# Indirect DMAs of GpSimd in another order and apart, from the last routing steps to the second expert's gathers

## The chip, the cores and the metric

The kernel runs on one core of a Trainium2 chip. The metric is the device time of one execution in microseconds (us), and the profile is that of one execution. TensorE (PE) multiplies, VectorE (DVE), ScalarE (ACT) and GpSimd (POOL) work on tiles in on-chip memory, and SyncE (SP) issues most of the plain DMAs. GpSimd also issues the indirect DMAs, whose row numbers come from a tile in on-chip memory.

## The reference

Two stages. The first is linear attention with a decay per head, in 12 blocks of 64 positions for 4 batches and 8 heads of 64. Its output, as 3072 rows of 512, goes through eight experts, each row through the one with the largest gate logit:

```python
intra = np.einsum('bhij,bhjd->bhid', np.einsum('bhic,bhjc->bhij', qb, kb) * Dmask, vb)
inter = np.einsum('bhid,bhde->bhie', qb * lam_pow, kv_state)
...
e_idx = np.argmax(x @ w_gate, axis=1)
gate_w = probs[np.arange(N), e_idx]
eom = 1.0 / (1.0 + np.exp(-(x @ w_output_gate)))
for e in range(E):
    mask = e_idx == e
    h = np.maximum(x[mask] @ w1[e], 0.0)
    out[mask] = gate_w[mask, None] * eom[mask, e, None] * (h @ w2[e])
```

## The kernel before

**Attention.** The 3072 rows are 24 tiles of 128 (6 chunks of positions by 4 batches). A loop over `s` from −2 to 21 is a software pipeline: in turn `s`, tile `s`+2 is loaded and turned (`stage_a`), tile `s`+1 has its scores (`stage_b`, L392, masked by VectorE into `at`, L401), and tile `s` its outputs (`stage_c1`, L416, and `stage_c`, L436, evicted into `xT`, L443). The order of the work on each engine is the order of the code. Behind the loop a tail does the last tile.

**Routing.** Tiles are routed in groups of four, the last four in pairs (`RES` is 16, `LAST` 20). For a group, `logits` multiplies (L484), `logit_rows` turns the result (ScalarE's `lT`, L488, TensorE's L495, VectorE's `lg`, L499), `route_choose` finds the expert (`oh`, L592) and `route_place` the place of each row among its expert's rows: ranks by TensorE (`pr`, L629 to L642), ten small operations of VectorE, and the index and the record of each tile in a list `pending`. `place_scatter` (L703) takes tiles from that list and writes their records into the table `tab_d` by an indirect DMA each (L708). `mark` (L604) compares slots with places, for `found`, with which TensorE finds expert 0's rows without the table.

**Gathers.** `gather` (L954) fetches 128 blocks of rows of x by one indirect DMA (L960) into `xg`. An expert has 14 of them. Expert 0's gathers 0 to 7 hold rows of the tiles ahead of 16 alone; 8 to 13 hold the late ones and wait for `row_join`. `row_index` turns the loaded table (`load_rows`, SyncE) into row numbers. `x_turn` (L977) turns gathered blocks into `y`, which expert 0's up matmuls read (L1012, `fill` runs some of them between the tail's steps). The up matmuls are evicted by ScalarE (`hhi`, L1031). L84 to L86 are down products, whose weights ScalarE casts to `whi` (L130).

**What sets GpSimd's order.** GpSimd executes in the order of the code. An indirect DMA holds it for about 1 us. `pace(t)` (L881) is a copy of one element of `t`, by which GpSimd waits until `t` is written. In the loop's turns 18 to 21 a gather follows a `pace` on the turn's `at`, another a `pace` on its `xT`, and in some turns a scatter follows. After the tail's chain there are four scatters, six gathers, fourteen gathers of the second expert (ten at once, four in `next_rows`), two sends of finished rows (L1163) and the third expert's gathers.

Of the kernel before, what the change touches and what calls it, by code (L numbers as in the profile page):

```python
# [25 lines left out]
def kernel(  # L26
# [673 lines left out]

    pending = []

    def place_scatter(count):  # L703
        for _ in range(min(count, len(pending))):
            idx, rec = pending.pop(0)
            scatter(
                "table",
                nc.gpsimd.indirect_dma_start(  # L708
                    out=tab_d,
                    out_offset=bass.IndirectOffsetOnAxis(ap=idx, axis=0),  # L710
                    in_=rec,
                    in_offset=None,
                    bounds_check=P * E * EB - 1,
                    oob_is_err=False,
                ),
            )

    def scatter(group, ins):
        inst = getattr(ins, "ins", ins)
        tc.declare_no_dep(inst, group=group, reason="these scatters write different rows")  # L720
        tc.add_to_no_dep_group(group, inst)
# [159 lines left out]
    def pace(t):  # L881
        nc.gpsimd.tensor_copy(out=beat, in_=t)

    def row_index(p, j0=0):
        if p >= E:
            return
        t, n = idxs[(p, j0)]
        gf = const.tile([32, 4 * n], F32, name=f"rowf_{p}_{j0}")
        nc.vector.scalar_tensor_tensor(
            out=gf, in0=t[:, :, 2], scalar=float(4 * NT), in1=t[:, :, 2], op0=ALU.is_lt, op1=ALU.mult  # L890
        )
        gi = const.tile([P, 4 * n], I32 if p else F32, name=f"rows_{p}_{j0}")
        for qq in range(4):
            nc.vector.tensor_scalar(
                out=gi[32 * qq : 32 * qq + 32], in0=gf, scalar1=float(P * qq), scalar2=None, op0=ALU.add
            )
        if p == 0:
            part0[j0] = gi
            return
        for b in range(4 * n):  # L900
            gis[(p, 4 * j0 + b)] = gi[:, b : b + 1]
# [49 lines left out]

    xg = {}

    def gather(p, b0=0, b1=None, rows=NT):  # L954
        if p >= E:
            return
        for b in range(b0, NB[p] if b1 is None else min(b1, NB[p])):
            if (p, b // 4) not in xg:
                xg[(p, b // 4)] = slot(f"xg_{p}_{b // 4}")
            nc.gpsimd.indirect_dma_start(  # L960
                out=xg[(p, b // 4)][:, (b % 4) * P : (b % 4 + 1) * P],
                out_offset=None,
                in_=x_q[0 : 4 * rows],
                in_offset=bass.IndirectOffsetOnAxis(ap=gis[(p, b)], axis=0),
                bounds_check=4 * rows - 1,
                oob_is_err=False,
            )
# [301 lines left out]
    with tc.manual_schedule():  # L1269
# [13 lines left out]
        for s in range(-2, NTILE - 2):  # L1283
# [45 lines left out]
            if s == RES + 1:  # L1329
                weave(len(later))  # L1330
                expert_regs(0, order_i, 1)
                place_scatter(B // 2)
            if s >= RES + 2:
                if s > RES + 2:
                    pace(live[s + 1]["at"][1][0:1, 0, 0:1])
                gather(0, 2 * (s - RES - 2), 2 * (s - RES - 2) + 1, RES * P)
            if 0 <= n < LAST:
                stage_d2(n)
            if s in STORES:
# [29 lines left out]
                load_piece(0)  # L1369
            if s >= RES + 2:  # L1370
                pace(xTs[s][0:1, 256:257])
                gather(0, 2 * (s - RES - 2) + 1, 2 * (s - RES - 2) + 2, RES * P)
                if s < RES + 4:
                    place_scatter(1)
                if s == RES + 5:
                    load_rows(0, 2)
                    load_piece(1)
# [6 lines left out]
        stage_b(n)  # L1384
        weave(2)
        stage_b2(n)
        stage_c(n - 1)
        logits(LAST, 2)
        weave(len(later))
        for b in range(B):  # L1390
            mark(RES, b, 1, late_width)
        place_scatter(len(pending))
        stage_c1(n)
        logit_rows(LAST)
        stage_c(n)
        at_once(route_choose(LAST, LAST + 2))
        place = route_place(LAST, LAST + 2)
        place[0]()
        place[-1]()
        x_turn(0, 0)  # L1400
        logits(LAST + 2, 2)
        stage_d2(n - 3, 2)
        fill(8)
        x_turn(0, 1)
        logit_rows(LAST + 2)
        fill(8)
        at_once(route_choose(LAST + 2, NTILE))
        stage_d2(n - 1, 2)
        load_piece(2)
        load_piece(3)  # L1410
# [6 lines left out]
            last[i]()  # L1417
        for b in range(2):
            mark(LAST + 2, b, 1, late_width)
        for f in place[1:-1]:  # L1420
            f()
        place_scatter(len(pending))
        for b in range(2):
            mark(LAST, b, 1, late_width)
        fill(10)
        pfound = bank("pfound_late")
        for n in range(RES, NTILE):
            found(pfound, n, (n - RES) // B + 1, late_width, n == RES, n == NTILE - 1)
        for i in (1, 3, 5, *range(7, len(last))):
            last[i]()  # L1430
        place_scatter(len(pending))
        settle(1)
        row_index(0, 2)
        fill(2)
        row_turn(2, pfound, late_width)
        row_join(2, late_width)
        gather(0, 8)
        settle()
        sort_rest(counts)
        row_counts()  # L1440
# [8 lines left out]
        for j in range(4):  # L1449
            split_quarter(3, j)  # L1450
            if j == 0:
                row_index(1)
                gather(1, 0, 10)
            fill(2)
            settle()
        fill(4)
# [22 lines left out]
        for p in range(E):  # L1479
# [5 lines left out]
            for fc in range(NFC):  # L1485
                if p == 0:
                    up(p, fc, 1)
                    if fc >= 4:
                        next_split(4, (fc - 4,))
                        for f in work[:2]:  # L1490
                            f()
                        work = work[2:]
                else:
                    up(p, fc)
                    next_split(4 * p + 2, (fc,))

                    if fc == 1 and p in TURNED:
                        out_index(p)
                    if fc == 3 and p == 2:
                        count_over()  # L1500
                    if fc >= 4:
                        for f in work[: (fc - 2) // 2]:
                            f()
                        work = work[(fc - 2) // 2 :]
                if fc == 3 and p in TURNED:
                    down_banks(p)
                if p == 0 and fc < 2:
                    next_rows(1, 10 + 2 * fc, 12 + 2 * fc)
                if p == 0 and fc == 2:
                    for ids, yn in held:  # L1510
                        send_rows(ids, yn)
                if p > 0:
                    b = (4 * 2 if p - 1 in TURNED else 2 * 2) + fc
                    next_rows(p + 1, b, 14 if fc == NFC - 1 else b + 1, hts[(p, fc)][0][0:1, 0:1].bitcast(F32))
                if fc == 0:
                    load_outs(p + 1)
                    load_rows(p + 2)
                if p - 1 in TURNED:
                    if fc == 2:
                        fetch_turned(p - 1)  # L1520
                    if fc >= 5:
                        send_turned(p - 1, fc - 5)
# [183 lines left out]
```

## Time and profile before

| what | us |
|---|---|
| median of 3 runs | 437.83 |
| lowest and highest | 436.9 and 438.7 |
| profiled execution | 437.95 |
| span of its profile | 435.9 |
| TensorE busy in the span | 406.9 |
| GpSimd busy | 237.6 |
| VectorE busy | 289.6 |
| ScalarE busy | 183.8 |

The span is the time from the first to the last instruction in the profile. A line of a time line has a start, a length, the engine, the line of the code, the operation with the tile that it writes and those that it reads, and in brackets the engine's idle time before it with what ended it. "issue" there means that nothing the profile shows was waited for. The granted clock of TensorE is given as a share of 2.4 GHz.

### The profile page before, as it was taken

How to read it: one execution, taken by the hardware profiler on the slowest of the kernel's cores; microseconds unless marked ns; L12 is line 12 of the kernel's file. 1: busy time of each engine (PE TensorE's matmuls, PEld its weight loads, DVE VectorE, ACT ScalarE, POOL GpSimd, SP SyncE). 2: the span in 40 equal slices, each digit the busy share in tenths (PEclk: the TensorE clock that was granted, in tenths of full speed). 3: DMA queues.
4: the chain of work that ended last, by engine and by line, in shares of the span. 5: the costliest groups of instructions: out<-in, count | busy, mean ns of one | idle time of the engine just before them, and what ended most of it. 6: DMA issues, size and time to landing. Idle time of an engine off the chain costs nothing.

```text
span 435.9 us, 10864 instructions
## 1 busy us (share of the span) xinstructions
PE 406.9 (93%) x3847; PEld 376.2 (86%) x3847; DVE 289.6 (66%) x852; ACT 183.8 (42%) x450; POOL 237.6 (55%) x323
## 2 busy tenths in 40 slices
PE   8899999987959789699999999999999999999995
PEld 5788889775839568589999999999999999999984
DVE  3767668594737442396767995796796796895611
ACT  3766666564411220254532551460461470471400
POOL 2478886766341747337657755654755755702302
PEclk9999999998868969699999999999999999999999
DMA  9999789989515516544447884784695695683301
GB/s 190 234 232 245 206 219 252 220 219 269 170 43 162 161 25 228 177 114 155 132 137 225 225 294 143 207 283 167 164 339 188 165 337 198 158 326 139 97 32 46
DMA packets 106287, 81.99 MB, mean 188 GB/s; under 512 B 67029, under 2 KB 81387, under 8 KB 106211
## 3 DMA queue, kind: packets, MB, share of 16 engines
q1 hardware_dynamic: 97666, 67.52, 53.8%
q0 software_dynamic: 6288, 13.12, 9.7%
q8 instruction: 52, 0.85, 0.8%
q10 hardware_dynamic: 2256, 0.30, 0.5%
q14 instruction: 25, 0.20, 0.1%
HBM read 63.78 MB, written 17.55 MB: 187 GB/s over the span
## 4 chain that ended last, share of the span: by engine, by line
PE 86%; issue 4%; DMA 3%; DVE 2%; SPq 2%; ACT 1%; another core or an unknown queue 1%; POOL 0%; ACTq 0%; POOLq 0%
PE ph L831 27%; PE py L831 23%; PE ph L1012 6%; PE po L436 5%; PE ps L392 5%; PE po L416 3%; PE pyr L84 2%; PE pk L344 2%; PE pyr L85 2%; PE pyr L86 2%; DMA qkv<-in_q_dram 2%; PE pq L344 2%; PE pl L484 2%; PE pst L449 2%
## 5 line engine op out<-in xcount | busy, mean ns | idle before, releaser
L960 POOL DMA_INDIRECT xg<-x_d,rows x103 | 114.4, 1111 | 69.0 <-issue 38.5
L1031 ACT ACTIVATE hhi<-ph 128x400 fp32r<-128x400 f32 (+6 forms) x72 | 33.5, 469 | 146.5 <-PE ph L831 96.5
L139 DVE TENSOR_TENSOR wlo<-raw,whi 128x512 fp32r<-128x512 f32 x120 | 79.7, 684 | 0.1
L831 PE MATMUL ph<-xhi,whi 128*128 128x400 f32 (+4 forms) x224 | 75.7, 338 | 0.0
L831 PE MATMUL ph<-xhi,wlo 128*128 128x422 f32 (+6 forms) x224 | 75.4, 337 | 0.0
L831 PE MATMUL ph<-xlo,whi 128*128 128x422 f32 (+6 forms) x224 | 75.2, 336 | 0.0
L130 ACT CAST whi<-raw 128x512 fp32r<-128x512 f32 x120 | 70.2, 615 | 5.6 <-DMA raw<-in_moe_w_dram 5.3
L1037 DVE SCALAR_TENSOR_TENSOR hlo<-ph,hhi 128x400 fp32r<-128x400 f32 (+6 forms) x72 | 37.1, 519 | 49.7 <-ACT hhi L1031 24.7
L831 PE MATMUL py<-hhi,whi 128*128 128x400 f32 (+9 forms) x192 | 65.1, 339 | 0.0
L831 PE MATMUL py<-hhi,wlo 128*128 128x422 f32 (+5 forms) x192 | 65.0, 338 | 0.0
L831 PE MATMUL py<-hlo,whi 128*128 128x422 f32 (+5 forms) x192 | 64.9, 338 | 0.0
L401 DVE TENSOR_TENSOR at<-ps,decay 128x512 f32<-128x512 f32 x48 | 31.3, 684 | 28.3 <-PE ps L392 23.3
L831 PEld LDWEIGHTS ph<-xlo,whi 128*128 128x128 f32 x224 | 42.2, 188 | 0.2
L831 PEld LDWEIGHTS ph<-xhi,wlo 128*128 128x128 f32 x224 | 42.1, 188 | 0.2
L831 PEld LDWEIGHTS ph<-xhi,whi 128*128 128x128 f32 x224 | 42.1, 188 | 0.2
L708 POOL DMA_INDIRECT tab_d<-rec,idx x24 | 24.7, 1028 | 24.1 <-DVE marks L604 15.5
L831 PEld LDWEIGHTS py<-hlo,whi 128*128 128x128 f32 x192 | 36.1, 188 | 0.2
L831 PEld LDWEIGHTS py<-hhi,wlo 128*128 128x128 f32 x192 | 36.1, 188 | 0.2
L831 PEld LDWEIGHTS py<-hhi,whi 128*128 128x128 f32 x192 | 36.0, 188 | 0.1
L352 ACT COPY qT<-pq 64x256 f32<-64x256 f32 x88 | 34.6, 393 | 2.1 <-PE pq L344 1.3
L1012 PE MATMUL ph<-y,raw 128*128 128x128 f32 (+2 forms) x160 | 30.7, 350 | 4.4 <-issue 4.4
L1012 PEld LDWEIGHTS ph<-y,raw 128*128 128x128 f32 x160 | 27.5, 216 | 7.1 <-issue 6.3
(215 smaller groups left out, 677.9 us busy)
## 6 DMA issues: line engine op xcount, KB each, us to landing
raw<-in_moe_w_dram SPq DMA_DIRECT2D x32, 1024.0 KB
x_d<-xn SPq DMA_DIRECT2D x12, 512.0 KB
qkv<-in_k_dram SPq DMA_DIRECT2D x38, 128.0 KB
qkv<-in_v_dram SPq DMA_DIRECT2D x19, 256.0 KB
qkv<-in_q_dram SPq DMA_DIRECT2D x36, 128.0 KB
yd<-yo SPq DMA_DIRECT2D x17, 256.0 KB
yr<-yd SPq DMA_DIRECT2D x68, 64.0 KB
xg<-x_d,rows POOLq DMA_INDIRECT x103
```

Of the source, the lines that this page charges most:

```text
L130: nc.scalar.copy(out=hi, in_=src)
L139: eng.tensor_tensor(out=lo, in0=src, in1=hi.bitcast(F32), op=ALU.subtract)
L352: copies = [lambda r=r, view=view, src=src: nc.scalar.copy(out=view(qT[r]), in_=src) for r, view, src in query_parts(pq)]
L392: nc.tensor.matmul(L["ps"][y][t, m * P : (m + 1) * P], L["kT"][r, m, t], L["qT"][r, m, :], start=True, stop=True)
L401: nc.vector.tensor_tensor(out=at, in0=ps.rearrange("p (g t) -> p g t", g=NPAIR), in1=dec[:, j], op=ALU.mult)
L436: nc.tensor.matmul(po[j * D : (j + 1) * D, i * P : (i + 1) * P], vt[:, 4 * y + m, :], L["at"][y][:, m, :], start=(c == 0), stop=(c == 0 or ...
L708: nc.gpsimd.indirect_dma_start(out=tab_d, out_offset=bass.IndirectOffsetOnAxis(ap=idx, axis=0), in_=rec, in_offset=None, bounds_check=P * ...
L831: nc.tensor.matmul(ps[:, 0:m], a[x], b[y][:, 0:m], start=first and i == 0, stop=last and i == 2)
L960: nc.gpsimd.indirect_dma_start(out=xg[(p, b // 4)][:, (b % 4) * P : (b % 4 + 1) * P], out_offset=None, in_=x_q[0 : 4 * rows], in_offset=ba ...
L1012: nc.tensor.matmul(phs[(p, fc)][:, r].rearrange("p (b r) -> p b r", b=nb), raws[fc // 4][:, kc, sl], ys[(p, h)][:, y0 : y0 + nb * P].rearr ...
L1031: nc.scalar.activation(out=hi[:, r], in_=ph[:, r], func=AF.Relu)
L1037: nc.vector.scalar_tensor_tensor(out=to, in0=ph[:, r], scalar=0.0, in1=hi[:, r].bitcast(F32), op0=ALU.max, op1=ALU.subtract,)
```

## The change

`idle_for(n)` is new: `n` copies of one element of the constant tile `warm`. `place_scatter` and `gather` take a count `rests` and put so many ahead of each DMA. With it and with `pace` the order of the indirect DMAs is another:

- Turn 17 has no scatter. Turns 18 to 21 have one gather and one scatter each, in place of two gathers and, in turns 18 and 19, one scatter.
- Gathers 4 to 7 of expert 0 stand in the tail. Gathers 4, 5 and 7 each stand behind a pace, on tile 23's `at` and on the last two `xT`; gather 6 stands behind a copy.
- The four scatters of tiles 16 to 19 come after gather 7, each behind a copy.
- The rest of `route_place` for tiles 20 and 21, its two scatters and two marks come ahead of `stage_d2(n - 3, 2)`, and `row_index(0, 2)` ahead of the last `logit_rows`; `x_turn(0, 1)` goes behind the last `route_choose`.
- The last two scatters, gathers 8 to 13 of expert 0 and all fourteen of expert 1 have a copy ahead of each.

```diff
-    def place_scatter(count):
+    def place_scatter(count, rests=0):
         for _ in range(min(count, len(pending))):
             idx, rec = pending.pop(0)
+            idle_for(rests)
...
+    def idle_for(count):
+        for _ in range(count):
+            pace(warm[0:1])
...
-    def gather(p, b0=0, b1=None, rows=NT):
+    def gather(p, b0=0, b1=None, rows=NT, rests=0):
...
+            idle_for(rests)
...
             if s == RES + 1:
                 weave(len(later))
                 expert_regs(0, order_i, 1)
-                place_scatter(B // 2)
             if s >= RES + 2:
                 if s > RES + 2:
                     pace(live[s + 1]["at"][1][0:1, 0, 0:1])
-                gather(0, 2 * (s - RES - 2), 2 * (s - RES - 2) + 1, RES * P)
+                gather(0, s - RES - 2, s - RES - 1, RES * P)
...
                 pace(xTs[s][0:1, 256:257])
-                gather(0, 2 * (s - RES - 2) + 1, 2 * (s - RES - 2) + 2, RES * P)
-                if s < RES + 4:
-                    place_scatter(1)
+                place_scatter(1)
...
         stage_b2(n)
+        pace(live[n]["at"][1][0:1, 0, 0:1])
+        gather(0, 4, 5, RES * P)
         stage_c(n - 1)
+        pace(xTs[n - 1][0:1, 256:257])
+        gather(0, 5, 6, RES * P)
         logits(LAST, 2)
         weave(len(later))
         for b in range(B):
             mark(RES, b, 1, late_width)
-        place_scatter(len(pending))
+        gather(0, 6, 7, RES * P, 1)
         stage_c1(n)
         logit_rows(LAST)
         stage_c(n)
+        pace(xTs[n][0:1, 256:257])
+        gather(0, 7, 8, RES * P)
+        place_scatter(len(pending), 1)
         at_once(route_choose(LAST, LAST + 2))
...
         logits(LAST + 2, 2)
+        for f in place[1:-1]:
+            f()
+        place_scatter(len(pending), 1)
+        for b in range(2):
+            mark(LAST, b, 1, late_width)
         stage_d2(n - 3, 2)
         fill(8)
-        x_turn(0, 1)
+        row_index(0, 2)
         logit_rows(LAST + 2)
         fill(8)
         at_once(route_choose(LAST + 2, NTILE))
+        x_turn(0, 1)
...
-        for f in place[1:-1]:
-            f()
-        place_scatter(len(pending))
-        for b in range(2):
-            mark(LAST, b, 1, late_width)
         fill(10)
...
-        place_scatter(len(pending))
+        place_scatter(len(pending), 1)
         settle(1)
-        row_index(0, 2)
...
-        gather(0, 8)
+        gather(0, 8, rests=1)
...
-                gather(1, 0, 10)
+                gather(1, 0, 10, rests=1)
...
-                    next_rows(1, 10 + 2 * fc, 12 + 2 * fc)
+                    gather(1, 10 + 2 * fc, 12 + 2 * fc, rests=1)
```

GpSimd, from turn 17's scatters to turn 20, before (`rec` is the record of a tile, `rows_0` the row numbers of expert 0's first gathers; x2 stands for two alike in a row):

```order
L708 DMA tab_d<-rec_868,idx_1912 24576x3 x2
L361 TENSOR_TENSOR qd_2118<-qT_2098,qdec 128x512
L960 DMA xg_0_2165<-x_d,rows_0_2162 128x128
L882 COPY beat<-xT_2170 1x1
L960 DMA xg_0_2165<-x_d,rows_0_2162 128x128
L708 DMA tab_d<-rec_868,idx_1912 24576x3
L882 COPY beat<-at_1_2260 1x1
L960 DMA xg_0_2165<-x_d,rows_0_2162 128x128
L882 COPY beat<-xT_2267 1x1
L960 DMA xg_0_2165<-x_d,rows_0_2162 128x128
L708 DMA tab_d<-rec_868,idx_1912 24576x3
L882 COPY beat<-at_1_2365 1x1
```

and after:

```order
L361 TENSOR_TENSOR qd_2112<-qT_2092,qdec 128x512
L966 DMA xg_0_2159<-x_d,rows_0_2156 128x128
L883 COPY beat<-xT_2164 1x1
L709 DMA tab_d<-rec_868,idx_1912 24576x3
L883 COPY beat<-at_1_2251 1x1
L966 DMA xg_0_2159<-x_d,rows_0_2156 128x128
L883 COPY beat<-xT_2258 1x1
L709 DMA tab_d<-rec_868,idx_1912 24576x3
L883 COPY beat<-at_1_2353 1x1
L966 DMA xg_0_2159<-x_d,rows_0_2156 128x128
```

Each indirect DMA now stands behind a copy of its own that waits for data of the turn, and the scatters are one to a turn.

GpSimd, from the loop's last gathers into the tail, before (`rec_957` is of tiles 16 to 19, `rec_1193` and `rec_1284` are of the last two pairs):

```order
L882 COPY beat<-at_1_2469 1x1
L960 DMA xg_1_2384<-x_d,rows_0_2162 128x128
L882 COPY beat<-xT_2480 1x1
L960 DMA xg_1_2384<-x_d,rows_0_2162 128x128
L708 DMA tab_d<-rec_957,idx_2382 24576x3 x4
L708 DMA tab_d<-rec_1193,idx_2608 24576x3 x2
L708 DMA tab_d<-rec_1284,idx_2678 24576x3 x2
L960 DMA xg_2_2781<-x_d,rows_2_2778 128x128 x4
L960 DMA xg_3_2794<-x_d,rows_2_2778 128x128 x2
L960 DMA xg_0_2941<-x_d,rows_0_2936 128x128 x4
```

and after:

```order
L883 COPY beat<-at_1_2516 1x1
L966 DMA xg_1_2519<-x_d,rows_0_2156 128x128
L883 COPY beat<-xT_2523 1x1
L966 DMA xg_1_2519<-x_d,rows_0_2156 128x128
L883 COPY beat<-warm 1x1
L966 DMA xg_1_2519<-x_d,rows_0_2156 128x128
L883 COPY beat<-xT_2571 1x1
L966 DMA xg_1_2519<-x_d,rows_0_2156 128x128
L883 COPY beat<-warm 1x1
L709 DMA tab_d<-rec_957,idx_2370 24576x3
L883 COPY beat<-warm 1x1
L709 DMA tab_d<-rec_957,idx_2370 24576x3
```

Gathers 4 to 7 now stand ahead of the four scatters of tiles 16 to 19, and no two DMAs stand side by side.

VectorE, between the one-hot of tiles 20 and 21 and the logits of tiles 22 and 23, before (`y` is what `x_turn` writes, `xn` the turned `xT` that is stored):

```order
L654 TENSOR_REDUCE oh_2613<-oh_2472 128x8
L977 STREAM_TRANSPOSE y_0_2615<-xg_0_2165 128x512
L519 STREAM_TRANSPOSE xn_2628<-xT_2390 128x512
L519 STREAM_TRANSPOSE xn_2628<-xT_2480 128x512
L977 STREAM_TRANSPOSE y_0_2615<-xg_1_2384 128x512
L499 TENSOR_REDUCE lg_2644<-pl_2617 128x32
```

and after, from the seventh of the moved operations on:

```order
L687 TENSOR_SCALAR den_2613<-pr_2617 128x2
L690 CAST idx_2616<-sl_2614 128x2
L691 SCALAR_TENSOR_TENSOR den_2613<-zs_2615,den_2613 128x2
L675 RECIPROCAL rec_1193<-den_2613 128x2
L604 TENSOR_SCALAR marks_2654<-slot_no,lead_143,sl_2614 128x192 x2
L519 STREAM_TRANSPOSE xn_2657<-xT_2377 128x512
L519 STREAM_TRANSPOSE xn_2657<-xT_2467 128x512
L894 SCALAR_TENSOR_TENSOR rowf_2_2671<-index_2_2482 32x8
L899 TENSOR_SCALAR rows_2_2673<-rowf_2_2671 32x8 x4
L499 TENSOR_REDUCE lg_2679<-pl_2625 128x32
```

The place of tiles 20 and 21, their marks and the row index stand ahead of the logits' reduction, and the turn of the second gathered block has left this place.

## Rows read from the trace of the kernel before

**Rows 1.** The page's first line, its span.

```profile
span 435.9 us, 10864 instructions
```

**Rows 2.** Busy time by stretch: PE, PEld, DVE, ACT, POOL, clock, DMA share, GB/s.

```profile
120.00:130.00 10.00, 4.80 (x64) 3.28 (x56) 3.24 (x14) 1.58 (x6) 5.16 (x6) 0.67 0.13 42
173.00:182.00 9.00, 4.57 (x16) 3.12 (x15) 0.79 (x5) 1.06 (x5) 4.88 (x5) 0.78 0.84 265
```

**Rows 3.** TensorE's waits, 100 to 195 us: total, times, longest.

```profile
PE ph L1012 <- issue: 4.4, 8, 1.0
PE pl L495 <- ACT lT L488: 3.0, 1, 3.0
PE pyr L84 <- issue: 2.9, 1, 2.9
PE pr L629 <- DVE oh L592: 2.2, 1, 2.2
PE po L416 <- issue: 1.6, 5, 0.3
PE pyr L84 <- ACT whi L130: 1.5, 1, 1.5
PE ps L392 <- issue: 1.5, 2, 0.8
```

**Rows 4.** Time line of GpSimd, first and last indirect DMA of four runs.

```profile
100.38 1.08 POOL L960 DMA_INDIRECT xg<-x_d,rows  x1 [2.35 <-ACT state L425]
...
107.24 1.02 POOL L708 DMA_INDIRECT tab_d<-rec,idx  x1 [0.30 <-issue]
...
118.95 1.03 POOL L960 DMA_INDIRECT xg<-x_d,rows  x1 [0.16 <-issue]
...
125.56 0.97 POOL L708 DMA_INDIRECT tab_d<-rec,idx  x1 [0.30 <-issue]
...
139.45 1.03 POOL L708 DMA_INDIRECT tab_d<-rec,idx  x1 [12.92 <-DVE marks L604]
...
151.19 1.00 POOL L960 DMA_INDIRECT xg<-x_d,rows  x1 [0.30 <-issue]
...
158.11 1.46 POOL L960 DMA_INDIRECT xg<-x_d,rows  x1 [5.93 <-issue]
...
178.10 1.00 POOL L1163 DMA_INDIRECT out_dram<-yn,table  x1 [0.30 <-issue]
```

**Rows 5.** Time line of VectorE, the two logits reductions of the tail.

```profile
127.60 0.22 DVE L499 TENSOR_REDUCE lg<-pl 128x32 f32<-128x64 f32 x1 [6.55 <-PE po L436]
...
133.95 0.22 DVE L499 TENSOR_REDUCE lg<-pl 128x32 f32<-128x64 f32 x1 [2.37 <-PE pl L495]
```

**Rows 6.** Time line of GpSimd, later gathers, some with copies between.

```profile
191.15 1.07 POOL L960 DMA_INDIRECT xg<-x_d,rows  x1 [12.05 <-PE pyr L86]
...
201.45 1.02 POOL L960 DMA_INDIRECT xg<-x_d,rows  x1 [0.16 <-issue]
...
206.02 1.28 POOL L960 DMA_INDIRECT xg<-x_d,rows  x1 [0.55 <-issue]
...
210.03 1.28 POOL L960 DMA_INDIRECT xg<-x_d,rows  x1 [0.54 <-issue]
```

**Rows 7.** Time line of ScalarE, two evictions beside these gathers.

```profile
201.71 0.53 ACT L1031 ACTIVATE hhi<-ph 128x432 fp32r<-128x432 f32 x1 [1.27 <-PE ph L831]
...
204.62 0.53 ACT L1031 ACTIVATE hhi<-ph 128x432 fp32r<-128x432 f32 x1 [1.88 <-PE ph L831]
```

**Rows 8.** Busy time in the stretches at half clock, the last of four and their sum.

```profile
178.00:184.80 6.80, 4.71 (x15) 4.45 (x15) 3.59 (x14) 2.58 (x8) 1.00 (x1) 0.50 0.31 110
sum 30.70, PE 23.06 PEld 18.96 DVE 14.30 ACT 8.23 POOL 8.08; mean PE 5.76 PEld 4.74 DVE 3.58 ACT 2.06 POOL 2.02
```

**Rows 9.** Time line of TensorE, up matmuls of the first and of the second piece.

```profile
133.74 2.84 PE L1012 MATMUL ph<-y,raw 128*128 128x128 f32 x24
...
141.53 5.80 PE L1012 MATMUL ph<-y,raw 128*128 128x256 f32 x26
```

## The prediction

> **What bounds the kernel now.** First the page: the span is 435.9 us [rows 1], the execution took 437.95, so 2.05 us lie around it, and the median of the runs shown, 437.83, is 0.1 lower. TensorE's line of the 40 slices is full from 195 us on; the gaps lie between 100 and 195, so whatever the change saves before 195 moves the end. Next, the busy time of that stretch [rows 2]: in 120 to 130 and 173 to 182 TensorE is busy for 4.80 of 10.00 and 4.57 of 9.00, at a granted clock of 0.67 and 0.78. Then the waits of TensorE [rows 3]. The longest group has no releaser at all ("issue"): 4.4 us in eight waits of the up matmuls L1012, 2.9 of L84, 1.6 of L416, 1.5 of L392. Two more, 3.0 for the turned logits and 2.2 for the one-hot, are the routing chain's. These six are 15.6 us.
>
> Last, GpSimd's own time line [rows 4]. Each group of waits lies beside an unbroken run of indirect DMAs whose starts are 1.3 us apart:
> - run 1, 100.38 to 107.24, six DMAs and three one-element copies between them, so 1.37 apart. L416 and L392 wait, 3.1.
> - run 2, 118.95 to 125.56, two gathers and four scatters. The logits and the one-hot wait, 5.2, and VectorE stands for 6.55 until 127.60 [rows 5].
> - run 3, 139.45 to 151.19, four scatters and six gathers, ten DMAs in 11.74, so 1.30 apart. L84 waits, 2.9, with no releaser.
> - run 4, 158.11 to 178.10, fourteen gathers and two sends. L1012 waits, 4.4, and all of it lies in 173 to 182.
>
> Elsewhere the kernel has DMAs further apart. From 206.02 to 210.03 there are two steps of 2.0 us, and nothing waits long. Around 201.45, where one copy stands between two of three neighbours, ScalarE stood idle for 1.88 ahead of 204.62 and for 1.27 ahead of 201.71 [rows 6, 7]: a delay of 0.6. So a run of DMAs goes together with engines that wait for nothing the profile names, and the longer and closer the run, the longer these waits. Why, the rows don't say. TensorE's clock adds to it: in four stretches of 30.70 us together, each behind such waits, the granted clock is 0.50, 1.2 GHz, with TensorE busy for 23.06 [rows 8]. At 2.4 GHz this work would be half, so 11.5 us are the ceiling of what the clock can give back, and the waits above are the ceiling of the rest.
>
> **The change part by part.** TensorE's, ScalarE's and SyncE's instructions keep their order and number. 52 copies and no DMA are added on GpSimd, and the DMAs are shared out anew.
> - *Run 1.* Tile 12's first two scatters move from ahead of the first gather to the places behind it, and a turn now holds one gather and one scatter in place of two gathers. Gathers 4 to 7 leave the loop. Two or so DMAs of six fall out of this stretch, a third of 3.1 or 1.0, and as those left have a wait on data between them, I take 1.5. Bounds 0 (six steps with copies in them stalled as well) and −3.1. Value −1.5.
> - *Run 2.* The four scatters behind one another leave; the end of the loop has one gather and one scatter, and the tail gets gather 4. About one DMA fewer in six near 120 and some waits on data: a fifth of 5.2. Value −1.1, bounds 0 and −5.2.
> - *What arrives at 126 to 137.* Gathers 5 to 7, the four scatters of tiles 16 to 19 and two of tiles 20 and 21 land where GpSimd had been idle for 12.92 us before 139.45 [rows 4]. That is nine DMAs in the routing chain's own stretch. Nothing in the trace of before has DMAs there; the nearest row is run 2's price in the same kind of chain, 5.2. The other bound is 0, as the first ones are each behind a copy that waits for a transposed block. I take a tenth, +0.5.
> - *VectorE's new order.* The ten small operations of tiles 20 and 21 with two marks and five row-index operations go ahead of the chain's second half. At 0.2 us each, as the row at 133.95 [rows 5], they are 3.4 together, and VectorE stands idle for 2.37 there, waiting for TensorE: 1.0 is not covered. In exchange the turn of the second block of gathered rows, a block of 128 x 512, goes behind the chain, and its first reader, the last third of the 24 up matmuls in the row at 133.74 [rows 9], may wait for it. I take these as even: value 0, bounds −0.5 and +1.0; without the idle time it would be +3.4.
> - *Run 3.* Eight of ten DMAs stay, two of the four scatters and gathers 8 to 13, each behind a copy; two scatters went ahead. With copies the step was 1.37 in run 1, against 1.30 here. TensorE's waits are 2.9, and 1.5 more for the weight cast that ScalarE, held up beside it, makes late [rows 3]: 4.4. Value −2.2, half of that; bounds 0 and −4.4.
> - *Run 4.* The same fourteen gathers, each behind a copy. Nothing else moves. The rows give an open answer: the copy adds 0.07 us to a step, next to nothing, but behind three DMAs with copies between the delay was 0.6, and behind six with copies, run 1, TensorE waited 3.1. Value −2.2, half of 4.4; bounds +2.5 and −4.4.
> - *The clock.* If one of the four stretches at 0.50 goes, it gives half of its busy time; the smallest, at 178.00, has 4.71 [rows 8]. Value −2.4, bounds 0 and −11.5.
> - *The copies themselves.* 22 gathers and scatters from 139 on get one. At 0.07 each that is 1.5 us on GpSimd, which stands idle for 12.05 ahead of 191.15 [rows 6], so nothing is late. Value 0. If each step grew to 2.0, as at 206.02 to 210.03, 22 × 0.7 = 15.4 would outrun that cover by 3.4.
> - *Loads on SyncE.* The second table load and a weight piece now wait for the last of tile 12's scatters, a few us later than before. The piece's first readers are the 256-column up matmuls from 141.53 on [rows 9], so 0.
>
> Sum: −1.5 − 1.1 + 0.5 − 2.2 − 2.2 − 2.4 = −8.9 against 437.95, so **429.05**, and 429 as a median.
>
> **The rivals.**
> - *The copies are what counts.* If a pause of any size lets the other engines through, all waits go, 15.6 and the 1.5 for the cast, and two of the four clock stretches with them, half of 11.5: 437.95 − 17.1 − 5.8 = 415. For it: delays are 0.6 where a copy stands between, against 2.9 and 4.4 where none does. Against it: run 1 had copies and stalled.
> - *Nothing changes but the place.* If the waits follow from the number of DMAs in the stretch 100 to 180, or come from somewhere else altogether and only lie beside the runs, the same DMAs give the same waits: 438. For it: no DMA is dropped, steps stay at 1.3 to 1.4, and run 1 had copies.
> - *The moved DMAs hold the routing chain.* Gathers 5 to 7 and six scatters sit in 126 to 137, where TensorE has only the chain logits, one-hot, ranks and short fills. If that costs as run 2 did, 5.2, and only run 1's 1.5 is gained, 437.95 + 5.2 − 1.5 = 441.6. It decides once its waits are over 9.4, if the other gains come as summed (8.9 and the 0.5 already in them), or over 2.6 if runs 1 and 2 alone give theirs. For it: run 2's waits are on just this chain. Against it: half of these DMAs stand behind copies that wait for late data, which spreads them. The Trainium skill (DMA: Bandwidth & Descriptors, Rules for kernel authors) speaks on this side: issue a transfer early and wait for it late. By it, taking gathers 4 to 7 later is a loss whatever the pauses do; no row shows what their reader would wait, as it is moved too.
> - *GpSimd becomes the bound.* Steps of 2.0 instead of 1.3 for 22 DMAs, less 12.05 of cover: 437.95 + 3.4 = 441.3. For it: the rows at 206.02 to 210.03. Against it: there the copies waited for the eviction whose tile they read, and the new ones read a constant.
>
> **How the numbers follow.** The forecast, relief in part, 0.42, with its own range of 421 to 435.5; full relief 0.18 (410 to 421); no effect 0.13; the chain held 0.17; GpSimd the bound 0.10. A measurement of this kernel can tell about 0.5%, 2.2 us. Faster by more: 0.42 + 0.18 = 0.60; within: 0.13; slower: 0.17 + 0.10 = 0.27. The range reaches into full relief, to 414, and to just above both slow cases, 442; about 0.09 is left out on either side, the parts of those cases with more than their price.
>
> **What would show it.** Right: in run 4's stretch L1012's waits without releaser fall below 3 us with the gathers still 1.3 to 1.4 apart; L84's near 150 fall by half; VectorE's 6.55 ahead of the first logits reduction shortens; one of the stretches at 0.50 is gone. Wrong: eight waits of some 4.4 us still beside the fourteen gathers mean that a copy does nothing; new waits of TensorE for the one-hot or the logits between 126 and 140 mean the third rival; gathers of the second expert that end after 195 mean the fourth. The sum fails most likely in the clock term, since a stretch at 0.50 comes or goes whole, and in the halves taken for runs 3 and 4.

## The result and the profile after

| | before | after |
|---|---|---|
| median, us | 437.57 | 425.73 |
| lowest and highest, us | 435.86 and 439.48 | 423.85 and 428.6 |
| ratio, 95% interval | | 0.9735 (0.9688 to 0.9783) |
| profiled execution, us | 437.95 | 423.85 |

The change makes the kernel 2.7% faster, 11.8 us; the forecast was 429.0 in a range of 414 to 442. The unedited change ran again on two of the chips below: on one it is 2.9% faster (425.13 against 437.89), and on the other, where the kernel before takes 408.39, it takes 414.07 and is slower by 1.5%. Both belong to the answer, and the experiments show where they come from. Times are compared only within one chip. Where some executions were disturbed (the order alone, the long copy), the ratio rests on the others and the median on all. The profiled execution of the change is the fastest of its six, 1.9 us under their median, so the terms read from it below are somewhat large.

The stretches of the profile after that answer to [rows 2] and [rows 8], with the same columns (length, busy time of PE, PEld, DVE, ACT and POOL, granted clock, DMA share, GB/s); those at 93.50, 120.60 and 168.60 are at half clock in the profile after:

```profile
120.00:130.00 10.00, 7.46 (x69) 6.50 (x69) 7.25 (x34) 1.87 (x8) 6.12 (x11) 0.83 0.48 176
173.00:182.00 9.00, 8.63 (x37) 5.96 (x36) 8.78 (x27) 6.77 (x18) 1.75 (x2) 1.00 0.35 114
...
93.50:96.70 3.20, 3.20 (x43) 2.49 (x39) 3.00 (x10) 1.00 (x4) 0.67 (x1) 0.50 0.86 200
120.60:124.10 3.50, 3.17 (x32) 2.63 (x36) 1.92 (x9) 1.04 (x5) 0.73 (x2) 0.53 0.87 327
154.10:160.90 6.80, 6.80 (x42) 6.68 (x41) 1.60 (x5) 0.66 (x2) 5.99 (x11) 1.00 0.83 283
168.60:172.00 3.40, 2.73 (x8) 2.15 (x7) 1.82 (x5) 0.84 (x2) 2.04 (x2) 0.50 0.44 147
```

Of the stretch at 154.10 the profile before has:

```profile
154.10:160.90 6.80, 5.95 (x13) 4.42 (x14) 4.69 (x12) 3.14 (x7) 2.45 (x2) 0.50 0.04 11
```

Half of 3.17 and of 2.73 is 2.9 us lost to the clock, and half of 3.20 another 1.6, together 4.5 where the four stretches of before lost 11.5 [rows 8]. The one at 93.50 begins ahead of the first instruction that the change touches. TensorE's waits between 100 and 195 us, to set beside [rows 3] (total, times, longest):

```profile
PE pl L495 <- ACT lT L488: 3.0, 1, 3.0
PE ph L1018 <- DVE oh L592: 1.7, 1, 1.7
PE ph L1018 <- issue: 1.5, 3, 1.0
PE pyr L84 <- issue: 1.1, 2, 0.7
PE pyr L85 <- issue: 0.9, 1, 0.9
PE pl L484 <- issue: 0.7, 2, 0.4
```

With three of 0.3 that are left out here they come to 9.8 us, against 17.5 before. Two places stand out. L84's 2.9 and the 1.5 for the weight cast near 150 are gone, all of it; the waits of L84 and L85 in this table lie at 166 to 170, beside the second expert's gathers. The wait for the turned logits, 3.0, is exactly as long as before, and a new one of 1.7 has come in the second half of the routing chain.

GpSimd's time line after, rows from the stretches that were runs 1 to 4:

```profile
101.13 1.12 POOL L966 DMA_INDIRECT xg<-x_d,rows  x1 [6.96 <-PE ps L392]
...
106.04 1.53 POOL L709 DMA_INDIRECT tab_d<-rec,idx  x1 [0.60 <-issue]
...
117.35 1.05 POOL L966 DMA_INDIRECT xg<-x_d,rows  x1 [0.15 <-PE pl L484]
...
125.79 1.04 POOL L709 DMA_INDIRECT tab_d<-rec,idx  x1 [0.17 <-issue]
...
132.46 0.98 POOL L709 DMA_INDIRECT tab_d<-rec,idx  x1 [0.16 <-issue]
...
139.73 1.06 POOL L966 DMA_INDIRECT xg<-x_d,rows  x1 [0.15 <-issue]
...
150.66 0.18 POOL L883 COPY beat<-warm 1x1 f32<-1x1 f32 x1
151.00 1.02 POOL L966 DMA_INDIRECT xg<-x_d,rows  x1 [0.16 <-issue]
152.03 0.18 POOL L883 COPY beat<-warm 1x1 f32<-1x1 f32 x1
152.37 1.03 POOL L966 DMA_INDIRECT xg<-x_d,rows  x1 [0.16 <-issue]
...
167.39 1.02 POOL L966 DMA_INDIRECT xg<-x_d,rows  x1 [0.16 <-issue]
```

A copy takes the place of the engine's idle time between two DMAs, so a step is 1.37 (151.00 to 152.37). Gather 8 starts at 139.73, where before it stood behind four scatters from 139.45 on [rows 4], and the second expert's gathers follow without the 5.93 us of idle time.

To see where the time went, the kernel is cut at four instructions of TensorE that every version has: the first matmul of `pfound`, the first of `pfound_late`, the first up matmul of expert 0's second half, and the first of the second expert. All are starts read from TensorE's time line, and the numbers are the us between two of them. From the last to TensorE's last matmul it is 235.8 to 236.4 us in all kernels of the table, so the end moves by what these stages move.

| kernel | pfound to pfound_late (runs 1, 2, the chain) | to expert 0's second half (run 3) | to the second expert (run 4) |
|---|---|---|---|
| before | 46.2 | 26.7 | 27.7 |
| change | 41.2 | 18.3 | 26.0 |
| change, run again on a chip that has the waits | 44.8 | 18.3 | 26.7 |
| change, on the chip without the waits | 36.9 | 18.3 | 19.6 |
| copies alone | 46.5 | 24.4 | 26.4 |
| change, but the loop as before | 47.0 | 18.3 | 25.3 |
| change, gathers and scatters exchanged | 39.6 | 25.4 | 26.1 |

Most of the gain, 8.3, is run 3's, 5.0 that of the loop and the chain, and 1.7 run 4's. In the change's second trace with the waits the first stage is 44.8, so its share there is smaller. In the last row `pfound_late` starts early and then waits inside, so its first two stages go together: 65.0, against 63.1 for the change on that chip.

### The profile page after: what moved, and what is told of

Same layout as the page of the kernel before. It is cut to its first block, busy times and chain, and to the rows that moved or that the text cites. A ratio compares the mean times of both kernels' runs of the same rounds, so it can differ in the third digit from the quotient of the medians.

```text
span 422.0 us, 10903 instructions
## 1 busy us (share of the span) xinstructions
PE 399.8 (95%) x3847; PEld 369.6 (88%) x3847; DVE 289.1 (69%) x852; ACT 183.7 (44%) x450; POOL 247.0 (59%) x355
## 4 chain that ended last, share of the span: by engine, by line
PE 84%; DMA 6%; DVE 3%; another core or an unknown queue 2%; issue 2%; SPq 1%; ACT 1%; POOL 0%; POOLq 0%; ACTq 0%; DVEq 0%
PE ph L832 28%; PE py L832 24%; PE ph L1018 6%; PE ps L392 4%; PE po L436 4%; DMA qkv<-in_k_dram 2%; PE po L416 2%; PE pl L484 2%; PE pk L344 2%; PE pyr L86 2%; PE pyr L84 2%; PE pyr L85 2%; PE pq L344 2%; DMA x_d<-xn 2%
## 5 line engine op out<-in xcount | busy, mean ns | idle before, releaser
L966 POOL DMA_INDIRECT xg<-x_d,rows x103 | 116.2, 1128 | 62.1 <-issue 27.3
L1018 PE MATMUL ph<-y,raw 128*128 128x128 f32 (+2 forms) x160 | 26.7, 319 | 3.4 <-DVE oh L592 1.7
L1018 PEld LDWEIGHTS ph<-y,raw 128*128 128x128 f32 x160 | 23.9, 190 | 5.1 <-issue 2.4
```

What stands on the lines that cost most here:

```text
L966: nc.gpsimd.indirect_dma_start(out=xg[(p, b // 4)][:, (b % 4) * P : (b % 4 + 1) * P], out_offset=None, in_=x_q[0 : 4 * rows], in_offset=ba ...
L1018: nc.tensor.matmul(phs[(p, fc)][:, r].rearrange("p (b r) -> p b r", b=nb), raws[fc // 4][:, kc, sl], ys[(p, h)][:, y0 : y0 + nb * P].rearr ...
```

## The experiments

The first theory, S, was that a pause between two indirect DMAs lets the other engines through; its rival, P, that only the places of the DMAs count.

**The order alone.** No copy of the constant tile; the paces on data stay.

```diff
     def idle_for(count):
         for _ in range(count):
-            pace(warm[0:1])
+            pass
```

> The changed order without any copy of the constant tile (the paces on data stay). Theory S, a copy between two indirect DMAs is what lets the other engines through: the gain from 139 us on is lost and the six scatters of the tail stand side by side, so TensorE's waits without releaser beside the second expert's gathers go from 2.4 us back to about 4.4 and the time is 431 to 434 us. Theory P, only the places of the DMAs count (fewer of them ahead of 125, and the fourteen gathers about 10 us earlier against the weight loads): 425 to 427 us, like the whole change.

Measured: 434.64 us (428.55 to 441.39) against 437.52, ratio 0.9845 (0.9756 to 0.9933). By the median of all four the order alone gains 2.9 us, a quarter of what the change does; by the ratio, which rests on two of them, something over half. It is far more scattered. The profiled execution is the longest of its four, so its rows show the waits at their largest. First TensorE, then VectorE, then GpSimd:

```profile
160.39 0.40 PE L86 MATMUL pyr<-whi,hlo 128*128 128x512 f32 x1
175.60 4.82 PE L1017 MATMUL ph<-y,raw 128*128 128x192 f32 x14 [14.82 <-DVE y L982]
```

```profile
152.21 1.90 DVE L139 TENSOR_TENSOR wlo<-raw,whi 128x512 fp32r<-128x512 f32 x3
173.76 0.75 DVE L1241 TENSOR_SCALAR yn<-pyr,table 128x512 f32<-128x512 f32 x1 [19.66 <-remote]
```

```profile
145.04 1.04 POOL L965 DMA_INDIRECT xg<-x_d,rows  x1 [3.73 <-PE ph L1017]
...
170.34 1.00 POOL L965 DMA_INDIRECT xg<-x_d,rows  x1 [0.30 <-issue]
```

VectorE stands still for 19.66 us. What it waits for is the product that TensorE ends at 160.79, and the trace's semaphore events have TensorE's update for it only at 173.74. From 145.04 on GpSimd issues its twenty gathers side by side, the last from 170.34 to 171.34. The gathers' own packets run and land all the while, each lot starting 1.7 us behind the start of its issue, and at 173.76 VectorE waits for none of them. What is late is the message from one engine to another. Whether the issue or the packets hold it up this does not tell: the last packets end at 173.17, 0.6 us ahead of the update.

**The copies alone.** The order of before, with a copy ahead of each scatter behind the loop and of the twenty gathers.

```diff
-        place_scatter(len(pending))
+        place_scatter(len(pending), 1)
...
-        gather(0, 8)
+        gather(0, 8, rests=1)
...
-                gather(1, 0, 10)
+                gather(1, 0, 10, rests=1)
```

> The order of before, with one copy ahead of each scatter behind the loop, of gathers 8 to 13 and of the second expert's fourteen gathers. Theory S: half of the waits of runs 3 and 4 goes, about 4.4 us, and a half-clock stretch with 2.4: 430 to 432 us. Theory P: 436 to 439 us, as before, with L1012's waits of some 4.4 us still beside the gathers.

Measured: 433.11 us against 437.52, ratio 0.9885 (0.985 to 0.992), 1.1 us above the range of S. TensorE's waits between 100 and 195 us:

```profile
PE pyr L84 <- ACT hhi L1037: 2.2, 1, 2.2
...
PE ph L1018 <- issue: 2.0, 6, 0.4
...
PE pyr L84 <- issue: 0.8, 1, 0.8
```

Beside run 4, 2.0 us stand where [rows 3] has 4.4; beside run 3, 0.8 and 2.2 for ScalarE's late eviction where it has 2.9 and 1.5. So the copies take off about half of run 4's and a third of run 3's waits without any move. P is out as the whole story: it had 425 to 427 us for the order alone and 436 to 439 for the copies alone. S came nearer, 0.6 and 1.1 us off, but a pause is not all either, as a third of run 3's waits goes by it and all of them with the move as well. The product of the two ratios, 0.9845 and 0.9885, is 0.973, the change's own; as the first rests on two executions, that may be chance.

**Run 4 without copies.** The whole change, but the second expert's gathers side by side.

```diff
-                gather(1, 0, 10, rests=1)
+                gather(1, 0, 10)
...
-                    gather(1, 10 + 2 * fc, 12 + 2 * fc, rests=1)
+                    gather(1, 10 + 2 * fc, 12 + 2 * fc)
```

> The whole change without the copies ahead of the second expert's fourteen gathers alone. Theory S: TensorE's waits beside them are 4.4 us again instead of 2.4, and a half-clock stretch comes with them: 428 to 431 us. Theory P: the gathers end 1 us sooner, the waits are 2.4 us or less: 424.5 to 426.5 us.

Measured: 430.17 us (426.18 to 433.83) against 437.52, too scattered for a ratio. The waits, of an execution of 427.54, tell more:

```profile
PE ph L1018 <- issue: 7.5, 11, 1.7
PE pl L495 <- ACT lT L488: 2.4, 1, 2.4
```

4.7 of the 7.5 lie at 163 to 172, beside these gathers and the two sends behind them. With the copies it is 2.4 there, in the profile after and in the change's second trace with the waits. Same place, same DMAs, steps of 1.30 in place of 1.37: S had 4.4, P 2.4 or less.

**Two copies for each one.**

```diff
-        for _ in range(count):
+        for _ in range(2 * count):
             pace(warm[0:1])
```

> The whole change with two copies in place of each one. Steps between the DMAs should be near 1.6 to 1.7 us. Theory S: the waits beside runs 3 and 4 go altogether, 2.4 us and the last half-clock stretch: 421 to 424 us. Theory P: the last gathers of the second expert move 5 us later, further into the weight loads from 154 us on, so 425 to 429 us.

Measured: 430.61 us against 437.52, ratio 0.9851 (0.9786 to 0.9916), above the ranges of S and of P, and a smaller gain than the change's 0.9735. The step was 1.98 and not 1.7: with a second copy GpSimd idles 0.54 ahead of the DMA. Time line of GpSimd, and then TensorE's waits:

```profile
162.55 1.03 POOL L966 DMA_INDIRECT xg<-x_d,rows  x1 [0.60 <-PE ph L1018]
163.57 0.41 POOL L883 COPY beat<-warm 1x1 f32<-1x1 f32 x2
164.53 1.02 POOL L966 DMA_INDIRECT xg<-x_d,rows  x1 [0.54 <-issue]
```

```profile
PE ph L832 <- issue: 5.5, 1, 5.5
PE ph L1018 <- DVE y L983: 3.9, 1, 3.9
PE ph L1018 <- DVE oh L592: 2.0, 1, 2.0
PE pl L484 <- issue: 1.7, 5, 0.4
```

Beside runs 3 and 4 no wait of L84 or L1018 without releaser is left. On one chip, then, run 4's waits without releaser are 4.7 at steps of 1.30, 2.0 at 1.37 (there in the order of before) and none at 1.98. In their place GpSimd is the bound: the last gathers end at 182 and the second expert's first matmul waits 5.5, and expert 0's second half waits 3.9 for its rows. These two are 9.4 us, the fourth rival, which counted 3.4 for the first alone.

**The change again, and three of its variants, on another chip.** These four ran together. The first is the change without an edit:

> The whole change once more, beside the next three on the same chip: 424 to 428 us by either theory.

The second has one copy of 256 elements, 0.39 us, in place of one element, for steps of 1.58:

```diff
-            pace(warm[0:1])
+            nc.gpsimd.tensor_copy(out=blank[0:1, 0:256], in_=blank[0:1, 256:512])
```

> The whole change with one longer copy (256 elements, some 0.4 us by the like copies of the trace) in place of each copy of one element, so steps near 1.6 us. Theory U, GpSimd's unbroken issue of indirect DMAs holds up the semaphore updates of the other engines and a longer pause lets them through: the second expert's gathers no longer go with waits without releaser (2.4 us and a half-clock stretch gone), GpSimd has 8.88 us of cover for some 6 us, so 421 to 424 us. Theory N, only the copy as such counts and not its length: 425 to 428 us, waits as after the change.

The third has two copies ahead of ten gathers alone:

```diff
-                gather(1, 0, 10, rests=1)
+                gather(1, 0, 10, rests=2)
```

> The whole change with two copies ahead of the second expert's first ten gathers, one elsewhere. Ten steps of 2.0 in place of 1.37 end the gathers 6 us later, within the 8.88 us for which GpSimd stood idle behind them. Theory U: no waits without releaser in that run, 422 to 425 us. If the weight loads beside the gathers make the waits, later gathers meet more of them: 427 to 430 us.

The fourth takes back the tail's moved steps:

```diff
         logits(LAST + 2, 2)
-        for f in place[1:-1]:
-            f()
-        place_scatter(len(pending), 1)
-        for b in range(2):
-            mark(LAST, b, 1, late_width)
         stage_d2(n - 3, 2)
         fill(8)
-        row_index(0, 2)
+        x_turn(0, 1)
...
         at_once(route_choose(LAST + 2, NTILE))
-        x_turn(0, 1)
```

> The whole change with the place of tiles 20 and 21, their scatters and marks, the row index and the second turn of gathered rows back where they were. If they had gone into VectorE's idle time at no cost and brought nothing but an earlier gather 8, the four scatters again stand together at 137 to 142 and gather 8 starts 2 to 3 us later: 427 to 429 us. If they held the routing chain (the third rival in part), without them 423 to 425 us.

| kernel | us | ratio to before, 408.39 us here |
|---|---|---|
| change | 414.07 | 1.0146 (1.0106 to 1.0186) |
| one long copy | 415.08 | 1.0157 (1.011 to 1.0203) |
| two copies ahead of ten gathers | 420.58 | 1.0305 (1.0266 to 1.0343) |
| tail's steps back | 414.41 | 1.0152 (1.0114 to 1.019) |

None of these expectations had this in it. The kernel before takes 29.1 us less here than on the chip of the runs above, and its granted clock is 0.992 to 1.000. No trace of it here was taken. Those of the change show what is absent: TensorE's waits between 100 and 195 us are, all of them,

```profile
PE ph L1018 <- DVE y L983: 3.9, 1, 3.9
PE pr L629 <- DVE oh L592: 0.5, 2, 0.3
PE ph L1018 <- PE pl L484: 0.2, 1, 0.2
```

Not one is without a releaser. And 29.1 is about what the waits and the clock of before come to, 17.5 and 11.5. That the kernel before has no waits here either is concluded from its time and its clock, not seen.

The same instructions on the two chips show the late message again. ScalarE's copy of the logits, first in the profile after, then in the one of this chip:

```profile
120.44 0.27 ACT L488 COPY lT<-pl 128x128 f32<-128x128 f32 x1 [2.68 <-remote]
```

```profile
115.81 0.27 ACT L488 COPY lT<-pl 128x128 f32<-128x128 f32 x1 [0.28 <-PE pl L484]
```

What it reads is done at 116.13 in the one (L484 from 115.49 for 0.64) and at 115.69 in the other (115.05 and 0.64); it starts 4.3 and 0.1 us later. In both GpSimd issues gathers at steps of 1.4 there (117.35, 118.75, 120.12 and 116.90, 118.29, 119.67), and both execute the same instructions with the same operands. The traces differ in one more thing: of the 1472 instructions by which TensorE, VectorE and ScalarE update their semaphores, 1251 have an event of their own in the profile before and 1242 in the one after, but 1460 in the change's trace on this chip. So the waits come with the chip, or with the occasion, as each chip was used once; where they occur, GpSimd's dense indirect DMAs bring them on.

What is likely to cost the 1.5% is in the same table of waits: 3.9 us for the second block of rows. TensorE, VectorE and GpSimd here:

```profile
126.67 2.08 PE L1018 MATMUL ph<-y,raw 128*128 128x128 f32 x8 [3.85 <-DVE y L983]
```

```profile
125.90 0.71 DVE L983 STREAM_TRANSPOSE y<-xg 128x512 f32<-128x512 f32 x1 [1.98 <-DMA xg<-x_d,rows]
```

```profile
121.03 1.02 POOL L966 DMA_INDIRECT xg<-x_d,rows  x1 [0.16 <-issue]
```

```profile
125.80:133.20 7.40, 6.53 (x38) 6.47 (x39) 4.17 (x17) 1.15 (x3) 5.74 (x11) 0.55 0.56 135
```

Gather 7, issued at 121.03, lands at 125.88 by its semaphore, VectorE is idle 1.98 for it and TensorE 3.85. Behind that wait the granted clock is 0.55 for 7.40 us, with 6.53 busy, some 2.9 lost. Together 6.8, near the 5.7 by which the change is slower; without a trace of before on this chip that is a comparison of sizes. This is the edit that the rule of the Trainium skill (DMA: Bandwidth & Descriptors, Rules for kernel authors), issue early and wait late, spoke against, and here the trace agrees with it. With the second turn of rows back ahead of the chain the time is the same, 414.41, as the rows are still late (TensorE waits 4.75 for them), so no cost of the tail's own moves shows here.

Two copies ahead of ten gathers give 6.5 us more than the change, with the second expert's first product late (TensorE's time line):

```profile
174.90 0.47 PE L832 MATMUL ph<-xhi,whi 128*128 128x432 f32 x1 [3.62 <-ACT xhi L997]
```

The long copy's question, whether steps of 1.58 would end the waits, stays open, as this chip has none; its time is that of the change.

**The kernel before again, and the change with the loop as before**, on a third chip. The first is without an edit:

> The kernel before, for its trace on the chip that these two runs get. If the waits without releaser belong to a chip and not to the kernel, then at some 408 us there are none of them between 100 and 195 us, no stretch at half clock beside GpSimd's four runs of indirect DMAs, and the same steps of 1.3 us between these; at some 437 us they stand as in the trace of before.

```diff
+                place_scatter(B // 2)
...
-                gather(0, s - RES - 2, s - RES - 1, RES * P)
+                gather(0, 2 * (s - RES - 2), 2 * (s - RES - 2) + 1, RES * P)
...
-        gather(0, 4, 5, RES * P)
...
-        gather(0, 7, 8, RES * P)
```

> The whole change with the gathers 0 to 7 and the scatters of tile 12's group back in the loop as before (two gathers in a turn), all else changed. If the change's loss where the waits don't occur comes from gathers 4 to 7 being late for the second block of rows (TensorE waits 3.9 us for it there), then where before takes some 408 us this takes 408 to 410. Where before takes some 437 us, half of the gain should be gone if fewer DMAs before 125 us are what helps: 430 to 433 us; if the copies and the spread scatters are all that helps, 425 to 428.

Measured: 435.0 in one execution for the first, whose trace has the waits again; 428.25 against 434.18 for the second, ratio 0.9851 (0.9775 to 0.9927). So with the loop's part undone a little over half of the result's gain is left, and the table of stages says where: the first stage is 47.0, as slow as before, the second 18.3, as fast as with the change. With the copies alone the second was 24.4. So run 3's waits go by the moved scatters and the copies together, and the first stage's by the loop: that stage is 39.9 to 44.8 in the traces with the change's loop on the chips with the waits, and 46.2 to 47.0 without it. (Apart from them, the profiled execution of the order alone, the longest of its four, has 48.1.)

**The change again, and gathers and scatters exchanged**, on a fourth chip: all eight first gathers in the loop, so that they are early, and tile 12's four scatters in the tail; the second turn of rows and the row index stand where they stood before.

> The whole change again, beside the next one. Where before takes some 435 us: 0.970 to 0.980 of it. Where before takes some 408 us: 1.010 to 1.018 of it, with TensorE waiting 3.9 us for the second block of rows.

```diff
                 pace(xTs[s][0:1, 256:257])
-                place_scatter(1)
+                gather(0, 2 * (s - RES - 2) + 1, 2 * (s - RES - 2) + 2, RES * P)
...
-        gather(0, 4, 5, RES * P)
+        place_scatter(1)
...
-        gather(0, 7, 8, RES * P)
+        place_scatter(1)
+        load_rows(0, 2)
+        load_piece(1)
```

> The whole change with gathers and scatters exchanged: all eight first gathers in turns 18 to 21, two to a turn behind paces, and the four scatters of tile 12's group in the tail at the places of gathers 4 to 7; the second turn of rows and the row index stand where they stood before. The number and the distances of the DMAs are as in the change. If the change loses by late gathers alone where the waits don't occur, and gains by distance alone where they do: at some 408 us of before 0.998 to 1.006 of it (no wait for the second block of rows), at some 435 us 0.968 to 0.980. If the scatters in the tail hold the table load and with it the last gathers, gather 8 starts 3 us or more later and this is slower than the change by 2 to 4 us.

Measured: the change 425.13 against 437.89, ratio 0.9714 (0.967 to 0.9758); the exchange 429.01, 0.9807 (0.977 to 0.9844). It keeps 9 of 13 us. The chip has the waits, so what it does without them stays open. GpSimd is held until the table load, and then eight scatters stand at steps of 1.31 with copies between; TensorE's come from 134.6 on:

```profile
127.92 0.98 POOL L709 DMA_INDIRECT tab_d<-rec,idx  x1 [3.58 <-DMA index<-tab_d]
...
137.12 0.98 POOL L709 DMA_INDIRECT tab_d<-rec,idx  x1 [0.16 <-issue]
```

```profile
136.54 0.24 PE L611 MATMUL pfound_late<-marks,row_lo 128*128 128x192 bf16 x1 [1.13 <-issue]
...
139.38 0.33 PE L612 MATMUL pfound_late<-marks,row_hi 128*128 128x192 bf16 x1 [0.96 <-issue]
```

This is the third branch of its expectation in size, 3.9 us slower than the change, but by another way: gather 8 is not late (141.44, and 141.41 in the change on this chip), and a run of eight scatters lies beside TensorE's work.

## Why the prediction came out

The direction was right, the gain of 11.8 a third larger than the 8.9 of the forecast, and the views that it rested on held: the waits without releaser beside GpSimd's runs of DMAs, and the clock behind them. A chip on which the kernel before is 29.1 us faster fits the two ceilings, waits and clock. By its terms, each in us of the profiled executions:

- **Run 1**, −1.5. Waits without releaser at 102 to 109 are 0.7, all L484's, where 3.1 stood: −2.4. Its half-clock stretch is gone.
- **Run 2**, −1.1. What was there fell from 5.2 to 3.5, −1.7, but not evenly: the wait for the logits is still 3.0, the one-hot's 2.2 is 0.2, and L416 has 0.3 beside it.
- **What arrives at 126 to 137**, +0.5, was too small. The second half of the chain now has 1.7 for the one-hot and 1.1 without releaser at 133 to 134, beside six scatters at steps of 1.33: +2.8. The third rival's mechanism is there, at half its price.
- **VectorE's new order**, 0, was not contradicted: taking it back moved nothing on the chip without waits, 414.41 against 414.07. On a chip with them it was not taken back.
- **Run 3**, −2.2, was half of what came. All 4.4 are gone, and with them the clock of the stretch at 154.10. The copies alone took about a third; the moved scatters with them took the rest, and the term did not weigh them enough.
- **Run 4**, −2.2: the waits at 165 to 170 are 2.4 where 4.4 stood, −2.0. Right.
- **The clock**, −2.4, was the term furthest off: 4.5 lost in place of 11.5, so −7.0. The text named it as the likeliest to fail, but for the reason that a stretch comes or goes whole, and that did not hold: two went, two shrank to 3.5 and 3.4 us, and one of 3.2 is new at 93.50. In the change's second trace with the waits four stretches lose some 7.5, so there the term is −4.0, and the waits are 11.5 in place of 17.5, −6.0:

```profile
sum 16.80, PE 15.32 PEld 12.70 DVE 7.36 ACT 5.82 POOL 4.70; mean PE 3.83 PEld 3.18 DVE 1.84 ACT 1.45 POOL 1.17
```

- **The copies' own price**, 0, was right at one copy. Of these 32 were added and not 52 (GpSimd has 323 instructions in the profile before and 355 after); the 22 of the term are right. The steps at 206.02 to 210.03 are 2.0 only on the mean, 1.76 and 2.25. The fourth rival's condition, steps of 2.0, came true with two, at 9.4 us and not 3.4, since expert 0's own rows are late as well.

With these the sum is −2.4 − 1.7 + 2.8 − 4.4 − 2.0 − 7.0 = −14.7, while the span fell by 13.9; 0.8 is not placed. So terms too small on both sides of the sum, the clock and run 3 on the one, what arrives at 126 on the other, partly made up for each other, and that the total came as near as it did is luck.

What failed is in none of the terms. Every rival took the waits for a property of the kernel. Where a chip doesn't have them, the change loses 1.5%, most likely by the late gathers, to which the prediction gave no price of their own, because their reader had been moved too.

## What to carry to other kernels

Waits without releaser on several engines at once, beside one engine's dense run of indirect DMAs, are worth a second look at where that run stands and how close its steps are: fewer in a run and a copy between gave 2.7% here, and neither part alone gave much over half of it. Count what such a wait does to the clock behind it, as that was 7.0 of 14.7 us in one profile and some 4 of 10 in another. And before an order is changed for a wait that no operand explains, run the kernel on a second chip: here the wait, and with it the sign of the result, changed from one to another.

## What the runs showed of the hardware

- Of the four chips of the experiments three had the waits (before at 437.52, 434.18 and 437.89 us) and one had none (408.39), with the same kernel; the change's steps between the DMAs are the same with and without them. What differs between the chips, or between the occasions, the runs don't show.
- Where they occur, a product that TensorE had ended at 160.79 had its semaphore updated at 173.74, 2.4 us after GpSimd's last DMA of the run had ended and 0.6 us after that DMA's last packets, while packets of the earlier ones ran and landed.
- In the traces with the waits some 85% of the updates of TensorE, VectorE and ScalarE have an event of their own (1251 and 1242 of 1472), in the one without them 99% (1460). Whether both have one cause is not shown.
- A copy of one element between two indirect DMAs lengthens a step from 1.30 to 1.37 us, a second one to 1.98.
